# Late stages of a fused backward pass: TensorE in program order, w_down gradient products between the dh tiles, earlier head-group loads

## The chip, the core and the metric

One core of one Trainium2 chip. The metric is the time of one execution on the device in microseconds (us); unless said otherwise a number is the median of several executions. A change counts as faster or slower from 2% on. Different sets of runs were taken on different chips, each beside runs of the kernel before on the same chip.

## The reference

The reference is a forward pass and its gradients. Attention over given caches is multiplied by a gated layer:

```python
def _A_ref(x, k_cache, v_cache, wq, wo):        # 32 heads of 128, 2048 rows, D = 576
    q = (x @ wq).reshape(B, Sq, H, Dh).transpose(0, 2, 1, 3)
    scores = einsum("bhqd,bhkd->bhqk", q, k_cache) * (Dh ** -0.5)
    o = einsum("bhqk,bhkd->bhqd", softmax(scores), v_cache)
    return o.transpose(0, 2, 1, 3).reshape(B, Sq, H * Dh) @ wo

def _B_ref(x, w_gate, w_up, w_down):            # F = 4608
    g, u = x @ w_gate, x @ w_up
    return (_sigmoid(g) * u) @ w_down

xn = _layernorm(x)
out = x + _A_ref(xn, ...) * _silu(_B_ref(xn, ...))
# outputs: out, and the gradients of x, k_cache, v_cache, wq, wo, w_gate, w_up, w_down
```

(Shortened; the reference writes the matrix products as einsums and takes the gradients with a vector-Jacobian product.)

## The kernel before

The change concerns what follows attention. First come the output rows. Then 18 blocks of 256 columns of the gated layer each compute dh, from it du and dg, then the gradients of w_down, w_up and w_gate, and the block's share of the gradient of x (the "dx rows"). Last, eight groups of four heads compute the gradients of wq and wo and their share of dx; there the tiles are called dq, on and ds. In this part the instructions of SyncE, GpSimd and VectorE stay in the order in which the program names them; those of TensorE and ScalarE are placed by the scheduler of the language.

```python
with ..., tc.manual_schedule(engines={SP, Pool, DVE}):          # shortened
    ...
    for fb in range(NFB):                                       # 18 blocks
        ...
        for st in range(0, NT, G2):                             # 8 steps of two row tiles
            dh = ps.tile([P, G2, FB], f32, name="dh")           # pool of two buffers
            for g in range(G2):
                srows = slice((st + g) * P, (st + g + 1) * P)
                for i in range(DT):                             # 5: so 10 matmuls of 256 columns
                    nc.tensor.matmul(dh[:, g, :], lhsT=doBT[:, i, srows], rhs=wdT[:, i, :], ...)
            nc.vector.tensor_tensor(du_blk[:, sp_, :], dh[:], a_blk[:, sp_, :], op=ALU.mult)
            nc.scalar.mul(ndh[:], dh[:], -1.0)
            nc.vector.tensor_tensor(dg_blk[:, sp_, :], ndh[:], nbl[:, sp_, :], op=ALU.mult)
            if e % NTQ == 0:                                    # after each half:
                for k in range(2):                              # duT, then dgT
                    turn_rows(dugT[k], dug[k], e - NTQ, e, FBT) # a DMA transpose on SyncE
        if fb == NFB - 1:
            nc.gpsimd.dma_start(ds_all, rows_view(ds_d, 0, D))  # ds load, last block only
        for fl in range(FBT):                                   # two w_down products
            accumulate(psa.tile(...), h_blk, doB, slice(fl * P, (fl + 1) * P), dwd)
            nc.gpsimd.dma_start(out_8[r0:r0 + P, :], dwd[:])
        if fb == NFB - 1:
            load_on(onb0, 0)                                    # on load of head group 0
        ...                                                     # up and gate products, dx rows
```

`accumulate` runs 16 row tiles, each a pair of matmuls of 512 and 64 columns, and ScalarE copies the sum out. A head group starts like this:

```python
for hg in range(NHG):                                           # 8 groups
    if not final:
        load_on(onqs[(hg + 1) % 2][0], hg + 1)                  # loads of the next group
        load_dq(onqs[(hg + 1) % 2][1], hg + 1)
    nc.sync.dma_start_transpose(wqT, A_wq[:, cols])
    for a in range(NTE if final else 0, NT, NQ):
        turn_rows(dqbT, dqb, a, min(a + NQ, NT), HG)            # four DMA transposes
    if early:                                                   # group 6
        nc.sync.dma_start_transpose(wqT2[:], A_wq[:, (hg + 1) * HC:(hg + 2) * HC])
        turn_rows(dqbT2, onqs[(hg + 1) % 2][1], 0, NTE, HG)     # group 7's tiles, for joined rows
    wait_n = min(4 if early else 2, nsteps - 2)                 # products before the first row ending
    ...
```

## Time and profile before

| | before |
|---|---|
| time, median of 3 | 4979.05 us (4975.73 to 4979.33) |
| span of the profiled execution | 4981.3 us |
| TensorE busy | 4857.5 us, 98% |
| start of the late part | 3533.30 us |
| output rows | 148.69 us |
| blocks 1 to 16 | 49.31 us each |
| head groups 1 to 5 | 47.04 us each |

The profile is of one execution. PE is TensorE's matmuls and PEld its weight loads; DVE, ACT, POOL and SP are VectorE, ScalarE, GpSimd and SyncE. A name such as `dh<-wdT,doBT` means that tile dh was written from wdT and doBT; L1098 is line 1098 of the kernel. Brackets hold the idle time ahead of an instruction and what ended it. The prediction shows the lines that matter. One more view is needed, the queues around the last block, with start, length, engine and transfer. The block starts at 4520.01:

```profile
4534.27 6.12 SPq L1047 DMA_TRANSPOSE duT<-du_blk  x1
4540.47 20.42 SPq L1047 DMA_TRANSPOSE dgT<-dg_blk  x1
```

```profile
4532.93 1.16 POOL L1115 DMA_DIRECT2D doBT<-ds_d  x1 [22.26 <-PE dh L1098]
...
4539.64 1.17 POOL L1026 DMA_DIRECT2D doB<-on_d  x1
```

The second dgT transpose (0.5 MB) is issued 0.83 us after the on load (2048 rows of 512 values of 2 bytes, 2.1 MB) and holds its queue for 20.42 us.

### The profile page before, as it was taken

The numbers are of one execution on the slowest core, as the hardware profiler recorded it, in microseconds if no ns is written. First come the engines' busy times: TensorE is split into PE (matmuls) and PEld (weight loads), VectorE is DVE, ScalarE is ACT, GpSimd is POOL, SyncE is SP. The second block draws the span as 40 slices with busy tenths as digits, with TensorE's granted clock in tenths as the row PEclk, the third lists the DMA queues.
The fourth block names the chain that finished last, engine by engine and source line by source line (L and its number), as shares of the span: only waits on it lengthen the run. The fifth ranks groups of instructions, "written<-read, shape, count | busy, mean of one in ns | idle before, by whom it ended". The sixth has DMA issues, their size and how long they took to land.

```text
span 4981.3 us, 100870 instructions
## 1 busy us (share of the span) xinstructions
PE 4857.5 (98%) x40276; PEld 2897.3 (58%) x41029; DVE 2790.1 (56%) x6554; ACT 2473.1 (50%) x4228; POOL 840.7 (17%) x1330
## 2 busy tenths in 40 slices
PE   9999999999999999999999999999899999999998
PEld 4445666666666666666666666665455555555454
DVE  4544665666666566566566666666334545453225
ACT  4422766766766766666676676676221111111111
POOL 3322111111111111111111111111221111111111
PEclk9999999999999999999999999999999999999999
DMA  7887999999999999999999999999999999998765
GB/s 260 273 204 173 224 229 225 226 233 228 225 229 221 229 227 225 228 232 230 224 225 237 222 231 226 230 225 224 206 224 235 230 212 228 214 222 160 207 167 146
DMA packets 3048180, 1097.68 MB, mean 220 GB/s; under 512 B 2951889, under 2 KB 2956114, under 8 KB 3047698
## 3 DMA queue, kind: packets, MB, share of 16 engines
q1 hardware_dynamic: 2948930, 771.66, 82.5%
q0 software_dynamic: 98160, 318.85, 20.3%
q8 instruction: 322, 5.28, 0.4%
q14 instruction: 160, 1.31, 0.1%
q10 hardware_dynamic: 608, 0.59, 0.0%
HBM read 175.31 MB, written 177.93 MB: 71 GB/s over the span
## 4 chain that ended last, share of the span: by engine, by line
PE 88%; DVE 4%; issue 3%; DMA 3%; ACT 2%; SPq 1%; POOL 0%; ACTq 0%; POOLq 0%; DVEq 0%
PE acc L683 18%; PE acc L744 17%; PE acc L997 11%; PE sp L636 8%; PE dp L706 8%; PE acc L1052 8%; PE acc L215 6%; PE u_ps L450 3%; PE g_ps L448 3%; PE acc L533 3%; PE acc L957 2%; DVE du_blk L1101 1%; ACT ndh L1103 1%; PE acct L145 1%; DMA dST<-Pq 1%
## 5 line engine op out<-in xcount | busy, mean ns | idle before, releaser
L654 ACT ACTIVATE Pq<-sp 128x1024 bf16<-128x1024 f32 x1024 | 1046.9, 1023 | 262.3 <-PE sp L636 219.2
L709 DVE SCALAR_TENSOR_TENSOR Pq<-dp,negdelta,Pq 128x1024 bf16<-128x1024 f32 x512 | 654.8, 1279 | 46.8 <-PE dp L706 46.6
L712 ACT ACTIVATE t<-dp,negdelta 128x1024 bf16<-128x1024 f32 x512 | 567.1, 1114 | 214.9 <-PE dp L706 165.0
L683 PEld LDWEIGHTS <-dST 128*128 128x128 bf16 x8192 | 508.3, 98 | 157.4 <-DMA dST<-Pq 16.9
L706 PE MATMUL dp<-VT,dOT 128*128 128x512 bf16 x1919 | 581.6, 379 | 2.3
L683 PEld LDWEIGHTS <-PT 128*128 128x128 bf16 x8192 | 500.1, 98 | 128.7 <-DMA PT<-Pq 8.6
L683 PE MATMUL acc<-Kn,dST 128*128 128x128 bf16 x8192 | 557.5, 219 | 13.6 <-DMA dST<-Pq 11.7
L636 PE MATMUL sp<-KQ 128*128 128x512 bf16 x1858 | 567.8, 379 | 2.2 <-ACT Pq L654 2.1
L683 PE MATMUL acc<-Vn,PT 128*128 128x128 bf16 x8192 | 542.1, 219 | 6.4 <-DMA PT<-Pq 4.4
L744 PE MATMUL acc<-Pq,dOn 128*128 128x512 bf16 x1983 | 527.8, 379 | 10.2 <-issue 0.2
L713 DVE TENSOR_TENSOR Pq<-t,Pq 128x1024 bf16<-128x1024 bf16 x512 | 354.4, 692 | 321.1 <-ACT t L712 306.3
L744 PE MATMUL acc<-Pq,Qn 128*128 128x512 bf16 x2013 | 523.7, 379 | 4.9
L1142 DVE TENSOR_TENSOR dxn<-acc,dxn 128x576 f32<-128x576 f32 x272 | 206.0, 757 | 316.9 <-PE acc L1052 316.9
L724 ACT ACTIVATE dq_n<-acc,rsc 128x128 bf16<-128x128 f32 x512 | 187.5, 366 | 339.4 <-PE acc L683 317.9
L744 PEld LDWEIGHTS <-Qn 128*128 128x128 bf16 x2048 | 200.3, 98 | 240.9 <-issue 1.6
L744 PEld LDWEIGHTS <-dOn 128*128 128x128 bf16 x2048 | 199.0, 98 | 234.6 <-issue 1.3
L1103 ACT ACTIVATE ndh<-dh 128x512 bf16<-128x512 f32 x144 | 86.0, 597 | 420.0 <-DVE du_blk L1101 419.9
L636 PEld LDWEIGHTS <-KQ 128*128 128x128 bf16 x2048 | 179.0, 98 | 123.8 <-issue 3.1
L706 PEld LDWEIGHTS <-dOT 128*128 128x128 bf16 x2048 | 178.8, 98 | 124.1 <-issue 11.7
L641 DVE TENSOR_REDUCE rs_all<-rsp 128x1 f32<-128x2 f32 x512 | 78.4, 153 | 306.5 <-ACT Pq L654 295.3
L677 POOL DMA_DIRECT2D on_d<-o_n x128 | 97.1, 759 | 778.7 <-DVE junk L695 458.9
L677 POOL DMA_DIRECT2D dq_d<-dq_n x128 | 97.9, 765 | 721.8 <-ACT dq_n L724 682.0
(209 smaller groups left out, 6800.1 us busy)
## 6 DMA issues: line engine op xcount, KB each, us to landing
out_dram<-kvn POOLq DMA_DIRECT2D x64, 512.0 KB, 3.9
ah<-a_d POOLq DMA_DIRECT2D x18, 1024.0 KB, 9.0
ah<-h_d POOLq DMA_DIRECT2D x18, 1024.0 KB, 10.8
h_d<-h_row POOLq DMA_DIRECT2D x64, 256.0 KB, 3.5
a_d<-a_row POOLq DMA_DIRECT2D x64, 256.0 KB, 3.8
x_all<-in_A_k_cache_dram SPq DMA_DIRECT2D x64, 256.0 KB, 3.8
on_d<-o_n POOLq DMA_DIRECT2D x128, 128.0 KB, 4.6
kvT_d<-KQ POOLq DMA_DIRECT2D x32, 512.0 KB, 5.4
```

What stands on the lines that cost most here:

```text
L215: nc.tensor.matmul(av[:, :CH], lhsT=w[:, i, :], rhs=srcT[:, i, cs], start=(i == 0), stop=(i == DT - 1))
L636: nc.tensor.matmul(sp[:, c * CH:(c + 1) * CH], lhsT=hs.QT[:, qt * P:(qt + 1) * P], rhs=hs.KT[:, hf * HW_ + c * CH: hf * HW_ + (c + 1) * CH ...
L654: nc.scalar.activation(Pq[:, hsl], sp[:], AF.Exp, scale=SCALE, accum_out=hs.rsp[:, hf:hf + 1])
L683: nc.tensor.matmul(hs.acc[:, 0, :], lhsT=T[:, kt, :], rhs=rhs[:, kt, :], start=(kt == 0), stop=(kt == NT - 1))
L706: nc.tensor.matmul(dp[:, c * CH:(c + 1) * CH], lhsT=hs.dOT[:, qt * P:(qt + 1) * P], rhs=hs.VT[:, hf * HW_ + c * CH: hf * HW_ + (c + 1) * C ...
L709: nc.vector.scalar_tensor_tensor(Pq[:, hsl], dp[:], hs.negdelta[:, qt:qt + 1], Pq[:, hsl], op0=ALU.add, op1=ALU.mult)
L712: nc.scalar.activation(t[:], dp[:], AF.Identity, bias=hs.negdelta[:, qt:qt + 1], scale=1.0)
L713: nc.vector.tensor_tensor(Pq[:, hsl], t[:], Pq[:, hsl], op=ALU.mult)
L744: nc.tensor.matmul(self.acc, lhsT=self.nat[:, qt, :], rhs=self.slabs[qt][:, cs], start=(qt == self.lo), stop=(qt == self.hi - 1))
L997: nc.tensor.matmul(acc[:, n0:n0 + nn], lhsT=lhs[:, st, cols], rhs=rhs[:, st, n0:n0 + nn], start=(st == 0), stop=(st == NT - 1))
L1052: nc.tensor.matmul(acc[:, n0:n0 + nn], lhsT=lT, rhs=w[:, n0:n0 + nn], start=(k == 0), stop=(k == len(terms) - 1))
L1142: nc.vector.tensor_tensor(dxn[:, st, :], acc[:, :D], dxn[:, st, :], op=ALU.add)
```

## The change

The intent is to let TensorE work on w_down gradient products while VectorE and ScalarE digest a dh tile, and to begin each head group's loads as soon as their buffers are free. Its core:

```diff
-            tc.manual_schedule(engines={SP, Pool, DVE}):
+            tc.manual_schedule(engines={SP, Pool, DVE, PE}):
...
-        def accumulate(acc, lhs, rhs, cols, dst):
-            for st in range(NT):
+        def accumulate(acc, lhs, rhs, cols, dst, a=0, b=NT):
+            for st in range(a, b):
...
+                dwd_units = [(fl, st) for fl in range(FBT) for st in range(NT)]
+                def dwd_unit():          # one row tile of one w_down product
+                    ...                  # after the last: copy out and store
                 for st in range(0, NT, G2):
...
                     nc.vector.tensor_tensor(dg_blk[...], ndh[:], nbl[...], op=ALU.mult)
+                    for _ in range(FBT * G2):
+                        dwd_unit()
...
                 if fb == NFB - 1:
                     nc.gpsimd.dma_start(ds_all, rows_view(ds_d, 0, D))
-                for fl in range(FBT):
-                    ...                  # the two w_down products and their stores
+                while dwd_units:
+                    dwd_unit()
...
+            if NHG > 1:                  # ahead of the head groups
+                load_on(onqs[1][0], 1)
+                load_dq(onqs[1][1], 1)
...
-                if not final:            # at the head of a group
-                    load_on(onqs[(hg + 1) % 2][0], hg + 1)
-                    load_dq(onqs[(hg + 1) % 2][1], hg + 1)
...
-                if early:                # behind the four dqbT transposes
-                    nc.sync.dma_start_transpose(wqT2[:], ...)
-                    turn_rows(dqbT2, ...)
...
-                wait_n = min(4 if early else 2, nsteps - 2)
+                wait_n = min(5 if early else 2, nsteps - 2)
...
                     nc.sync.dma_start_transpose(dwq[:, :, lcols], dqTs[h % 2][:])
+                    if early and hl == min(1, HG - 1):
+                        nc.sync.dma_start_transpose(wqT2[:], ...)
+                        turn_rows(dqbT2, ...)
...
                 if not final:            # after a group's products
+                    if hg + 2 < NHG:
+                        load_on(onb, hg + 2)
+                        load_dq(dqb, hg + 2)
```

(Tile names and some arguments are shortened.) A consequence in the last block: the last w_down store is now emitted ahead of the ds load.

More of the change, by code (lines that the diff above doesn't have):

```diff
@@ L882 @@
     with late("pc") as pc, late("pcf") as pcf, \
-            tc.manual_schedule(engines={mybir.EngineType.SP, mybir.EngineType.Pool, mybir.EngineType.DVE}):
+            tc.manual_schedule(engines={mybir.EngineType.SP, mybir.EngineType.Pool, mybir.EngineType.DVE, mybir.EngineType.PE}):
         xn_all = pc.tile([P, NT, D], bf, name="xn_all")
@@ L998, in accumulate @@
                                      start=(st == 0), stop=(st == NT - 1))
-            alt.copy(dst[:, :D], acc[:, :D], eng="s")
+            if b == NT:
+                alt.copy(dst[:, :D], acc[:, :D], eng="s")
         def store_T(out_, cols, stg_):
@@ L1089 @@
                 du_blk, dg_blk = dug
+                dwd_units = [(fl, st) for fl in range(FBT) for st in range(NT)]
+                dwd_box = []
+                def dwd_unit():
+                    fl, st = dwd_units.pop(0)
+                    if st == 0:
+                        dwd_box[:] = [outp.tile([P, D], bf, name="dwd"), psa.tile([P, WD], f32, name="acc", tag="acc")]
+                    accumulate(dwd_box[1], h_blk, doB, slice(fl * P, (fl + 1) * P), dwd_box[0], st, st + 1)
+                    if st == NT - 1:
+                        r0 = fb * FB + fl * P
+                        nc.gpsimd.dma_start(out_8[r0:r0 + P, :], dwd_box[0][:])
                 for st in range(0, NT, G2):
@@ L1115 @@
                     nc.gpsimd.dma_start(ds_all, rows_view(ds_d, 0, D))
-                for fl in range(FBT):
-                    dwd = outp.tile([P, D], bf, name="dwd")
-                    accumulate(psa.tile([P, WD], f32, name="acc", tag="acc"), h_blk, doB, slice(fl * P, (fl + 1) * P), dwd)
-                    r0 = fb * FB + fl * P
-                    nc.gpsimd.dma_start(out_8[r0:r0 + P, :], dwd[:])
+                while dwd_units:
+                    dwd_unit()
                 if fb == NFB - 1:
@@ L1203 @@
                     turn_rows(dqbT, dqb, a, min(a + NQ, NT), HG)
-                if early:
-                    nc.sync.dma_start_transpose(wqT2[:], A_wq[:, (hg + 1) * HC:(hg + 2) * HC])
-                    turn_rows(dqbT2, onqs[(hg + 1) % 2][1], 0, NTE, HG)
                 dwq = wp.tile([P, DT, HC], bf, name="dwq")
@@ L1227 @@
                     nc.sync.dma_start_transpose(dwq[:, :, lcols], dqTs[h % 2][:])
+                    if early and hl == min(1, HG - 1):
+                        nc.sync.dma_start_transpose(wqT2[:], A_wq[:, (hg + 1) * HC:(hg + 2) * HC])
+                        turn_rows(dqbT2, onqs[(hg + 1) % 2][1], 0, NTE, HG)
                     if final and hl == HG - 1:
```

## The prediction

> **What bounds the kernel now.** I read the page first, then busy times by stage, then the timeline of TensorE, and last the waits of the queues. The page says that TensorE is the engine that matters:
>
> ```profile
> PE 4857.5 (98%) x40276; PEld 2897.3 (58%) x41029; DVE 2790.1 (56%) x6554; ACT 2473.1 (50%) x4228; POOL 840.7 (17%) x1330
> ```
>
> With 98% busy there can be no large gain from order alone. The change touches only what follows attention: a stage of output rows (about 3533 to 3682 us), 18 blocks of the gated-layer gradients (3682 to 4576) and 8 head groups (4576 to the end at 4981). So I looked for time lost there. One steady block is 4224.17 to 4273.47, 49.30 us, and the next ones repeat it to 0.01 us. Busy time of its three parts (dh with the w_down products; up and gate products; dx rows; columns: stretch, length, then PE, PEld, DVE, ACT, POOL, granted clock, DMA share, GB/s):
>
> ```profile
> 4224.17:4242.11 17.94, 17.37 (x143) 11.95 (x145) 11.62 (x22) 5.31 (x9) 0.56 (x1) 1.00 1.01 214
> 4242.11:4257.79 15.68, 15.58 (x128) 8.06 (x129) 2.24 (x4) 2.55 (x4) 2.93 (x5) 1.00 0.94 215
> 4257.79:4273.47 15.68, 15.52 (x127) 8.06 (x129) 11.36 (x15) 0.64 (x1) 4.76 (x6) 1.00 0.97 283
> ```
>
> Second and third part are dense: a pair of matmuls (512 and 64 columns) takes 0.245 us start to start (15.68 us / 64 pairs). A w_down, up or gate product over 16 row tiles is 16 pairs, 3.92 us; a dx row is 4 pairs, 0.98 us. A dh tile is 10 matmuls of 256 columns, 1.09 us (the first 20 of the block start 2.18 us before what follows). So the first part should be 8 x 1.09 + 2 x 3.92 = 16.56 us and takes 17.94: **1.38 us are lost per block**. The timeline of TensorE shows how:
>
> ```profile
> 4230.39 1.25 PE L1098 MATMUL dh<-wdT,doBT 128*128 128x256 bf16 x10
> 4231.48 0.65 PE L997 MATMUL acc<-doB,ah 128*128 128x64 bf16 x4
> 4232.14 1.25 PE L1098 MATMUL dh<-wdT,doBT 128*128 128x256 bf16 x10
> ...
> 4236.72 5.55 PE L997 MATMUL acc<-doB,ah 128*128 128x512 bf16 x43
> ```
>
> dh tiles come every 1.75 us with only about two pairs (0.49 us) between; 1.09 + 0.49 leaves some 0.17 us unused per tile, and the remaining w_down work is piled up at the end. The 1.75 us is the chain of VectorE and ScalarE, in program order on VectorE, with two dh buffers:
>
> ```profile
> 4227.22 0.68 DVE L1101 TENSOR_TENSOR du_blk<-dh,ah 128x512 bf16<-128x512 f32 x1
> 4228.62 0.42 DVE L1104 TENSOR_TENSOR dg_blk<-ndh,nbl 128x512 bf16<-128x512 bf16 x1 [0.72 <-ACT ndh L1103]
> 4228.96 0.68 DVE L1101 TENSOR_TENSOR du_blk<-dh,ah 128x512 bf16<-128x512 f32 x1
> ```
>
> Outside the blocks the chain breaks in three places: at the last block's dx rows, at group 0's dx rows, and in group 6, the last but one, where dx rows of two groups are joined:
>
> ```profile
> 4563.72 0.66 PE L1052 MATMUL acc<-wug,duT 128*128 128x512 bf16 x4 [2.08 <-DMA duT<-du_blk]
> 4566.56 0.74 PE L1052 MATMUL acc<-wug,dgT 128*128 128x64 bf16 x3 [2.18 <-DMA dgT<-dg_blk]
> ...
> 4612.41 17.51 PE L1052 MATMUL acc<-wdT,dqbT 128*128 128x512 bf16 x126 [4.71 <-ACT dqT L40]
> ...
> 4886.69 2.10 PE L1052 MATMUL acc<-wqT,dqbT 128*128 128x512 bf16 x8 [4.90 <-DMA dqbT<-dqb]
> ```
>
> Groups 1 to 5 are dense: 47.04 us each, which is 8 x 3.92 + 16 x 0.98.
>
> **What the Trainium skill says.** (1) "TensorE: Matmul & The Clock Gate", Part 2, step by step: matmuls keep program order, only weight loads are pulled ahead. The trace agrees: one weight load of the next dh tile runs at 4226.57, its other nine from 4226.89, when the tile's matmuls may start. So the emitted order is the whole lever. (2) "PSUM — Partial Sum Buffer", PSUM bank collisions: two engines must not touch one bank at once, so software keeps them apart. The trace agrees: ndh waits for du_blk although both only read dh (419.9 us of waiting in 142 places); the 1.75 us chain stays as it is. (3) The TensorE page, Part 1: after an idle window of about 3.4 us the clock falls to half until it has been busy as long. The trace agrees: after the 4.90 us wait eight matmuls take 1.92 us instead of 0.98. (4) "DMA: Bandwidth & Descriptors", Issuing engines are not separate DMA queues: all share 16 engines. The trace agrees: one dgT transpose issues in 1.98 us in the quiet first half of the last block, and holds its queue 20.42 us beside the ds and on loads.
>
> **The change part by part.**
> *w_down units among the dh tiles.* Work is neither added nor removed: 32 units of one pair, four after each dh tile. A step becomes 1.09 + 4 x 0.245 = 2.07 us, longer than the 1.75 us chain, so a dh buffer is free before TensorE needs it (du_blk, ndh and their handoffs take about 1.6 us after a tile's end; the tile two later starts 3.05 us after it). The old trace already shows such steps in block 0, at 3692.03, 3694.10 and 3696.17: 2.07 us. First part 16.56 us, block 47.92 us, saving 1.38 x 17 blocks = **23.5 us**. Block 0 has an extra VectorE multiply per step and gets nothing from me. The up product starts 0.98 us after the last dh tile and reaches the last rows some 3.4 us later, after du_blk; second-half transposes finish about 18 us after a block's start plus 4 us landing, against 40 us when dx needs them. Neither waits.
>
> *Last block.* It lost 22.54 - 15.68 = 6.86 us in its dx rows. The new order puts the last w_down store ahead of the ds load, so that load starts about 18 us into the block instead of 12.9; the second duT transpose (about 16.7) is then ahead of it, but dgT (about 18.3) still runs beside it. If dgT needs the 25.7 us it needed before, it lands at 44 where 40 is the need: half of the loss stays. I take **3.5 us** gain.
>
> *Group 0.* Loss now 4.71 us, plus 17.51 - 0.16 - 15.68 = 1.7 us at the low clock. The wait is named for ScalarE, but its cause is the queue: four dqbT transposes hold it for 32.58 us beside two 2 MB loads, and the dwq transposes behind them free dqT. Both loads are now emitted before the group. The on load was stuck behind the dwg store, which comes earlier when the last block's queue flows, so only one load would collide. I give it 60%: **4 us**.
>
> *Groups 1 to 5.* Already dense; the loads were issued during the previous group's dx rows at 4664, 4711, 4758 and are again. **0 us.**
>
> *Group 6.* Before, from its start 4864.96: transposes of both groups end at 19.1 us, and the join starts at 21.7. Now two dwq transposes (second ready at 12.6) come before the second set, so wqT2 goes out at about 15.8, dqbT2 at 18.0, and lands near 24.7, while TensorE is there after five products, 19.6. The wait stays about 5 us and the eight row endings on VectorE, 4.36 us each, start 3 us later: **2 us loss**. Group 7 and the tail: as before.
>
> *Output rows.* TensorE waits 10.5 us for a wo load and 3.5 us for the third oT; program order can use the first gap, but the third oT lands at the same time. **0 us.**
>
> Sum: 23.5 + 3.5 + 4 - 2 = 29 us; 4979 - 29 = **4950 us**, 0.6% less.
>
> **The rivals.**
> *DMA becomes the bound of the blocks.* For it: DMA share 0.92 to 0.99 in steady blocks, and a block 2.8% shorter would want up to 1.02. Against it: the same measure reaches 1.08 elsewhere, transposes land in 4 us, and TensorE waits for no DMA in any steady block. It would leave 0 to 10 us of the 23.5: 4963 to 4973.
> *Program order shows waits that the old order hid.* A wait in each block of 1.4 us would cancel everything: about 4975; a wait of 5 us in a few groups would cost 10 to 20 us: 4960 to 4970. For it: ScalarE is still ordered by the scheduler, and the join stands before data that may be late. Against it: the old order is nearly the program order already, outside the dh part.
> *The boundary stalls vanish altogether,* since transposes are now spaced differently: the 6.9, 6.4 and about 8 us (4.9 plus the slow clock) all go, 23.5 + 21 = 45 us: 4935.
>
> **Range and chances.** The 23.5 us is nearly arithmetic; the rest is -5 to +15 us of DMA timing. Range 4938 to 4963 us. Two per cent are 100 us, more than all idle time of TensorE in these stages, so faster by over 2% gets 0.01; slower by over 2% needs a stall of 7 us in every block, 0.01.
>
> **What would show it.** Right: steady block 47.92 us, dh steps of 2.07 us with eight matmuls between, no wait of L1098 for ndh; on load of group 1 before the last dx row ends; group 6 with a wait of some 5 us at its first joined row. Wrong: a block longer than 48.5 us, or TensorE waiting for duT, dgT, wug or wdT in steady blocks.

## The result, and the profile after

| | before | after |
|---|---|---|
| median | 4977.39 us (4 runs, 4973.89 to 4979.33) | 4948.19 us (4 runs, 4946.58 to 4964.82) |
| ratio | | 0.995, 95% interval 0.9927 to 0.9972 |
| profiled span | 4981.3 us | 4944.8 us |

The kernel after is 0.5% faster, which is within 2%: the class that had 0.98. The median is 1.8 us under the predicted 4950.

The page's busy time of the kernel after, with the same columns as before:

```profile
PE 4874.4 (99%) x41029; PEld 2893.5 (59%) x41029; DVE 2801.6 (57%) x6554; ACT 2474.9 (50%) x4228; POOL 842.3 (17%) x1330
```

The busy sums do not settle the matter: the trace before holds 40276 matmul records and this one 41029, so part of the 17 us rise on PE is records missing before. The stages do. A steady block of the kernel after, in its three parts (stretch, length, then PE, PEld, DVE, ACT, POOL, granted clock, DMA share, GB/s):

```profile
4206.89:4223.46 16.57, 16.57 (x147) 11.87 (x145) 9.27 (x16) 4.71 (x8) 1.08 (x2) 1.00 1.13 249
4223.46:4239.14 15.68, 15.68 (x131) 8.06 (x129) 5.24 (x9) 3.04 (x5) 1.63 (x3) 1.00 1.10 222
4239.14:4254.82 15.68, 15.68 (x131) 8.06 (x129) 11.36 (x15) 0.64 (x1) 6.03 (x8) 1.00 1.11 279
```

TensorE is busy in all of it. The 17.94 us of the first part have become 16.57, the others kept their 15.68. The timeline of TensorE shows the steps:

```profile
4208.96 1.26 PE L1110 MATMUL dh<-wdT,doBT 128*128 128x256 bf16 x10
4210.05 1.14 PE L997 MATMUL acc<-doB,ah 128*128 128x512 bf16 x8
4211.03 1.26 PE L1110 MATMUL dh<-wdT,doBT 128*128 128x256 bf16 x10
...
4223.46 2.83 PE L997 MATMUL acc<-xn_all,du_blk 128*128 128x512 bf16 x21
```

The dh tiles start 2.07 us apart, with eight matmuls between, and no w_down work is left over at the end. The chain of VectorE no longer sets the pace, since each du_blk now waits for TensorE:

```profile
4210.25 0.69 DVE L1113 TENSOR_TENSOR du_blk<-dh,ah 128x512 bf16<-128x512 f32 x1 [0.23 <-PE dh L1110]
4211.66 0.43 DVE L1116 TENSOR_TENSOR dg_blk<-ndh,nbl 128x512 bf16<-128x512 bf16 x1 [0.72 <-ACT ndh L1115]
4212.32 0.69 DVE L1113 TENSOR_TENSOR du_blk<-dh,ah 128x512 bf16<-128x512 f32 x1 [0.23 <-PE dh L1110]
```

What TensorE's matmuls and weight loads of dh tiles waited for, over the whole run, first before, then after (us, times):

```profile
  issue: 30.5, 104
  ACT ndh L1103: 4.0, 18
```

```profile
  issue: 2.1, 5
  ACT ndh L1115: 0.8, 2
```

"Issue" is a wait for nothing that the profile names; before it stood ahead of the second weight load of a dh tile, 104 times. It has all but gone with the waits for ndh.

In the last block, which now starts at 4494.48, the second pair of transposes is issued ahead of both loads (ds at 18.53 us into the block, on at 19.69), and dgT holds its queue for 3.97 us:

```profile
4511.00 1.43 SPq L1048 DMA_TRANSPOSE duT<-du_blk  x1
4512.52 3.97 SPq L1048 DMA_TRANSPOSE dgT<-dg_blk  x1
```

Group 6 got longer. In the kernel after it starts at 4824.66. A joined row is eight matmuls of group 6 (dqbT with the tile named wdT here) and eight of group 7 (with wqT). The first row's second half, which needs group 7's transposes, and the start of the next row:

```profile
4849.29 2.10 PE L1053 MATMUL acc<-wqT,dqbT 128*128 128x512 bf16 x8 [3.89 <-DMA dqbT<-dqb]
4851.21 1.85 PE L1053 MATMUL acc<-wdT,dqbT 128*128 128x512 bf16 x8
```

That is 24.63 us into the group, where before it was 4886.69 - 4864.96 = 21.73. The wait itself shrank, from 4.90 to 3.89 us. The group got longer at its end, where TensorE waits for the row endings on VectorE, which run later: once for 2.23 us and once for 2.79, against one wait of 1.68 before.

```profile
4887.14 5.56 PE L1053 MATMUL acc<-wdT,dqbT 128*128 128x512 bf16 x32 [2.79 <-DVE dxn L1256]
```

The eight matmuls take 4851.21 - 4849.29 = 1.92 us in place of 0.98, as they did before after 4.90 us of waiting. That again agrees with the clock behaviour which the prediction quotes from the Trainium skill: 3.89 us is a little over its idle window of about 3.4 us. The granted clock also shows where that short statement is too simple. The half-speed spell lasts 3.41 us here, but 6.83 us in group 6 of the kernel before. And in the dx rows of the kernel before, half speed set in at 4564.80 around two waits of 2.08 and 2.18 us with 0.66 us of work between them, neither of which is as long as the window.

All stages of these two profiles, and of three more of the same two kernels that the experiments gave (e10 and e12 are the kernel before again, e8 is the kernel after again), in us:

| stage | before | before, e10 | before, e12 | after | after, e8 |
|---|---|---|---|---|---|
| start of the late part | 3533.30 | 3530.30 | 3535.20 | 3532.07 | 3541.69 |
| output rows | 148.69 | 152.63 | 152.09 | 145.42 | 152.82 |
| block 0 | 49.12 | 49.13 | 49.13 | 50.06 | 50.07 |
| blocks 1 to 16 | 788.90 | 789.03 | 789.06 | 766.93 | 766.93 |
| block 17 to its dx rows | 33.63 | 33.64 | 33.64 | 32.26 | 32.26 |
| its dx rows | 22.54 | 16.86 | 15.68 | 15.68 | 15.68 |
| group 0 | 53.58 | 47.04 | 47.04 | 47.04 | 47.04 |
| groups 1 to 5 | 235.20 | 235.20 | 235.20 | 235.20 | 235.20 |
| groups 6, 7 and the tail | 116.34 | 116.77 | 116.46 | 120.14 | 119.91 |
| from the first dh tile to the end | 1299.31 | 1287.67 | 1286.21 | 1267.31 | 1267.09 |

Read from the first two profiles alone (before, after), blocks 1 to 16 gave 22 us, the last block's dx rows 6.9, group 0 6.5. The other columns correct that: the last two come and go in one and the same kernel.

### The profile page after: what moved, and what is told of

It is laid out like the page before. It is cut to its first block, busy times and chain, and to the rows that moved or that the text cites. A ratio compares the mean times of both kernels' runs of the same rounds, so it can differ in the third digit from the quotient of the medians.

```text
span 4944.8 us, 101626 instructions
## 1 busy us (share of the span) xinstructions
PE 4874.4 (99%) x41029; PEld 2893.5 (59%) x41029; DVE 2801.6 (57%) x6554; ACT 2474.9 (50%) x4228; POOL 842.3 (17%) x1330
## 5 line engine op out<-in xcount | busy, mean ns | idle before, releaser
L636 PE MATMUL sp<-KQ 128*128 128x512 bf16 x2048 | 609.7, 379 | 2.2 <-ACT Pq L654 2.1
L706 PE MATMUL dp<-VT,dOT 128*128 128x512 bf16 x2048 | 609.2, 379 | 2.3
```

Of the source, the lines that this page charges most:

```text
L636: nc.tensor.matmul(sp[:, c * CH:(c + 1) * CH], lhsT=hs.QT[:, qt * P:(qt + 1) * P], rhs=hs.KT[:, hf * HW_ + c * CH: hf * HW_ + (c + 1) * CH ...
L706: nc.tensor.matmul(dp[:, c * CH:(c + 1) * CH], lhsT=hs.dOT[:, qt * P:(qt + 1) * P], rhs=hs.VT[:, hf * HW_ + c * CH: hf * HW_ + (c + 1) * C ...
```

## The experiments

Twelve runs followed, all correct; e8, e10 and e12 are the kernel after or before once more. "Stages" below means the profile's stages as in the table.

| run | median us | its kernel before | ratio, 95% |
|---|---|---|---|
| e1_order_only | 5024.0 | 4979.0 | 1.0084 (1.0052 to 1.0116) |
| e2_blocks_only | 4945.9 | 4979.0 | 0.9928 (0.9896 to 0.9960) |
| e3_units_scheduled | 4951.97 | 4979.0 | 0.9937 (0.9905 to 0.9969) |
| e4_ds_late | 4973.99 | 4979.0 | 0.9984 (0.9951 to 1.0017) |
| e8_after_again | 4961.07 | 4977.43 | 0.9961 (0.9933 to 0.9988) |
| e5_ds_early | 4956.19 | 4977.43 | 0.9955 (0.9928 to 0.9982) |
| e6_join_early | 4947.04 | 4977.43 | 0.9932 (0.9904 to 0.9960) |
| e9_halves | 4935.95 | 4977.43 | 0.9913 (0.9883 to 0.9943) |
| e10_before_again | 4978.49 | 4980.22 | 0.9999 (0.9982 to 1.0016) |
| e7_on_late | 4979.5 | 4980.22 | 1.0004 (0.9987 to 1.0020) |
| e11_dgt_behind | 4962.97 | 4980.22 | 0.9967 (0.9951 to 0.9984) |
| e12_before_third | 4973.77 | 4982.77 | 0.9986 (0.9952 to 1.0020) |

### Which part of the change does the work

**e1, program order on TensorE alone:** the kernel before with

```diff
-            tc.manual_schedule(engines={SP, Pool, DVE}):
+            tc.manual_schedule(engines={SP, Pool, DVE, PE}):
```

> The kernel before with TensorE in program order and nothing else. My theory: the gain of the blocks comes from w_down pairs standing between the dh tiles, so without them TensorE waits for the 1.75 us chain of VectorE and ScalarE: last dh tile ends about 12.5 us into a block as before, the two w_down products (7.84 us) follow, first part 20.4 us, block about 51.7 us instead of 49.30, in all 4977 + 17 x 2.45 = about 5019 us. Rival, program order by itself is the gain: block 48 us, about 4950 us.

It is slower by 45 us in the medians, as expected. Blocks 1 to 16 take 51.77 us each and block 0 60.98. TensorE in a steady block:

```profile
4309.51 1.25 PE L1098 MATMUL dh<-wdT,doBT 128*128 128x256 bf16 x10 [0.38 <-ACT ndh L1103]
4311.26 1.25 PE L1098 MATMUL dh<-wdT,doBT 128*128 128x256 bf16 x10 [0.50 <-ACT ndh L1103]
...
4319.35 8.00 PE L997 MATMUL acc<-doB,ah 128*128 128x512 bf16 x62
```

The dh tiles again come every 1.75 us, now with nothing between, and the whole w_down work stands behind them. So 1.75 us is the pace of the chain through VectorE and ScalarE, and the scheduler's two pairs between the tiles had hidden part of it.

**e2, the blocks without the head-group part:** the kernel after with the loads, `wait_n` and the wqT2 and dqbT2 transposes of the head groups as before.

```diff
-            if NHG > 1:
-                load_on(onqs[1][0], 1)
-                load_dq(onqs[1][1], 1)
...
+                if not final:
+                    load_on(onqs[(hg + 1) % 2][0], hg + 1)
+                    load_dq(onqs[(hg + 1) % 2][1], hg + 1)
...
-                wait_n = min(5 if early else 2, nsteps - 2)
+                wait_n = min(4 if early else 2, nsteps - 2)
...                                       # wqT2 and dqbT2 back behind the dqbT transposes
```

> The change without its head-group part (loads of the groups, place of the joined transposes, and row start are as before); TensorE in program order, w_down pairs among the dh tiles. My theory: block 47.93 us; the last block and group 0 run dense (15.68 us of dx rows, 47.04 us) because of the block part alone; group 6 back to about 64.6 us from 67.9: about 4945 us, 3 below the full change. Rival, the loads moved by the head-group part freed group 0: group 0 waits 4 to 6 us again, 4951 to 4955 us.

Blocks 47.93 us, the last block's dx rows and group 0 together 62.7 as in the kernel after, groups 6, 7 and tail 115.11. The whole gain is in the blocks. The head-group part gives nothing and costs 120.14 - 115.11 = 5.0 us at the end in these two profiles; e3 below, with the same head groups as e2, took 117.0 there, so 3 to 5 us. The part holds three edits (loads, `wait_n`, place of the transposes), which e2 takes back together.

**e3, the same with TensorE left to the scheduler:** e2 with

```diff
-            tc.manual_schedule(engines={SP, Pool, DVE, PE}):
+            tc.manual_schedule(engines={SP, Pool, DVE}):
```

> As e2_blocks_only, but TensorE is left to the scheduler. The emitted order of TensorE in the blocks turns out to be the same. My theory: program order by itself brings nothing once the pairs are written between the tiles; block 47.93 us, within 3 us of e2_blocks_only, about 4945 us; only the first output rows are ordered otherwise. Rival, program order brings the 3.3 us seen in the output rows: those rows take 148.7 us here against 145.4 in e2_blocks_only.

Blocks 47.93 us as well. Once the w_down units are emitted between the tiles, the scheduler keeps them there, so fixing TensorE's order isn't needed for the gain. The time was 6 us above e2's, and the output rows took 154.87 us against 145.61. That is in the direction of the rival, but e5 and e6, with TensorE in program order, took 154.30 and 153.43 us there, so this doesn't show that program order speeds these rows up. One more line of this profile matters later. In the last block, which starts at 4504.07, dgT was issued at the same place as in the kernel after, 0.50 us ahead of the ds load, and yet:

```profile
4522.10 14.50 SPq L1048 DMA_TRANSPOSE dgT<-dg_blk  x1
```

### Where the last block's stall came from, and whether it was there

**e4, only the ds load moved:** the kernel before with the ds load behind the w_down stores.

```diff
-                if fb == NFB - 1:
-                    nc.gpsimd.dma_start(ds_all, rows_view(ds_d, 0, D))
                 for fl in range(FBT):
                     ...                  # w_down product and store
+                if fb == NFB - 1:
+                    nc.gpsimd.dma_start(ds_all, rows_view(ds_d, 0, D))
                 if fb == NFB - 1:
                     load_on(onb0, 0)
```

> The kernel before with one load moved: the ds load of the last block is issued after the two w_down stores instead of before them; TensorE's order is unchanged. My theory: the waits at the last block's dx rows (6.9 us with the low clock) and at group 0 (6.5 us) came from the ds load running ahead of the last du transpose, so both go: 4977 - 13 = 4964 us with blocks still 49.30 us. Rival, they went because of the denser blocks or because of the loads of the head groups: 4977 us, dx rows of the last block again 22 us.

Both transposes now go ahead of the loads: duT held its queue for 1.43 us (6.12 before), dgT, at 15.78 us into the block, for 3.20 (20.42 before). Dx rows 15.68, group 0 47.04, so the 13.4 us of stalls in the first profile are absent. But the time fell by only 5 us, with an interval that holds 0. The output rows took 154.61 us here, with the same instruction order on TensorE as before.

**e8, the kernel after again,** unchanged.

> The changed kernel once more, on the chip of the next three runs, to compare with them and to see how far its first output rows (145.4 us in its first profile) vary: 4948 us, stages 47.93 us a block, 47.04 us group 0, some 120 us from group 6 to the end. If the output rows vary by chance of transfer order they may take up to 150 us.

From the first dh tile to the end it repeats to 0.2 us (table above). The late part started 9.6 us later and the output rows took 152.82 us against 145.42. So the 3.3 us that the rows had "gained" were chance.

**e5, the ds load early in the new order:** the kernel after with the ds load behind the last dh tile instead of behind the last w_down store, 0.57 us ahead of the second duT transpose.

```diff
+                    if fb == NFB - 1 and st == NT - G2:
+                        nc.gpsimd.dma_start(ds_all, rows_view(ds_d, 0, D))
                     for _ in range(FBT * G2):
                         dwd_unit()
...
-                if fb == NFB - 1:
-                    nc.gpsimd.dma_start(ds_all, rows_view(ds_d, 0, D))
```

> The changed kernel with the ds load of the last block issued where the last dh tile frees its buffer (about 15.8 us into the block), ahead of the last duT transpose (16.5), as in the kernel before. My theory: duT then takes some 6 us to issue, dgT comes behind the on load (18.6) and takes some 20 us; the last block's dx rows take 20 to 23 us again and group 0 50 to 54: 4948 + 13 = 4961 us. Rival, the denser blocks or the earlier group loads removed these waits: 4948 us.

The expected stall did not come: dx rows 15.68, group 0 47.04. The transposes did slow down: duT held the queue for 12.93 us in place of 1.43, and dgT could only start at 29.53 us into the block and ended at 33.9. The second half of the dx rows needs it at about 40. A slow transpose is a stall only when its slack is used up.

**e7, the other load moved:** the kernel before with the on load of group 0 behind the first dwu stores, so that nothing is issued just ahead of the second dgT transpose.

```diff
-                if fb == NFB - 1:
-                    load_on(onb0, 0)
                 kv_store()
                 for (blk_, out_, nm) in (...):
                     ...
                     store_T(out_, fcols, stg_)
+                        if fb == NFB - 1:      # after nm == "dwu"
+                            load_on(onb0, 0)
```

> The kernel before with the on load of group 0 moved behind the first w_down gradient stores of the last block; everything else in its order. Theory (a transpose issued within a microsecond or so behind a 2 MB load goes slowly): the second dgT transpose, issued at about 20.5 us, now has no load close ahead of it and takes about 7 us in place of 20.4, so dx rows 15.7 and group 0 47.0: 13.4 us less in the profile's stages, ratio about 0.997. Rival (the ds load of 4 MB ahead is what slows it): the stall stays, dx 22 and group 0 53, ratio 1.000.

(The text calls the ds load 4 MB; by its shape, 2048 rows of 576 values of 2 bytes, it is 2.36 MB.) Dx rows 15.68 and group 0 47.04. The queue, in a block that starts at 4522.75:

```profile
4537.02 6.36 SPq L1047 DMA_TRANSPOSE duT<-du_blk  x1
4543.47 7.61 SPq L1047 DMA_TRANSPOSE dgT<-dg_blk  x1
```

With the ds load where it was and the on load away, dgT holds the queue for 7.61 us. That speaks for the on load just ahead of it as what made it slow, and against the ds load. In e1 too, dgT was issued ahead of the on load, 8 us behind the ds load, and held its queue for 7.02 us. But these are two profiles, and in e3 dgT took 14.50 us with both loads behind it, so the load just ahead is not the only cause. The time, however, did not move at all, and the next two runs give a reason.

**e10 and e12, the kernel before again,** unchanged, with a profile each.

> The kernel before once more, with a profile of its own: how far do the parts that my theory uses repeat? Theory: the stalls of the last block belong to the order in which its loads are issued and repeat: dx rows about 22.5 us, group 0 about 53.6, blocks 49.3 each, while the output rows (145 to 155 in the runs so far) and the start of the late part (3532 to 3544) are chance. Rival: the stalls of the last block are chance too, and dx rows or group 0 come at 15.7 and 47.0. Time within 0.4% of the kernel before.

> A third profile of the kernel before, unchanged. The first one lost 6.9 us in the last block's dx rows and 6.5 us in group 0; the second, of the same code, lost 1.2 us and 0.0. Theory formed on that: how long the transpose behind the 2 MB on load takes differs from execution to execution, near 20 us, around the 40 us at which dx needs it, so the loss lies anywhere from 0 to 13 us and a third profile will show dx rows between 15.7 and 22 us and group 0 mostly at 47.0. Rival: the second profile was the odd one, and dx rows are 22 and group 0 53 again. Blocks 1 to 16 at 49.31 us each in both.

The same two transposes, first of e10 (its block starts at 4521.09), then of e12 (4525.48):

```profile
4535.35 6.34 SPq L1047 DMA_TRANSPOSE duT<-du_blk  x1
4541.78 17.17 SPq L1047 DMA_TRANSPOSE dgT<-dg_blk  x1
```

```profile
4539.75 6.37 SPq L1047 DMA_TRANSPOSE duT<-du_blk  x1
4546.21 13.01 SPq L1047 DMA_TRANSPOSE dgT<-dg_blk  x1
```

One code, issued at the same moment of the block to within 0.3 us, and dgT holds the queue for 20.42, 17.17 and 13.01 us. TensorE in e10 waits only once in the dx rows:

```profile
4564.23 0.66 PE L1052 MATMUL acc<-wug,dgT 128*128 128x512 bf16 x4 [1.01 <-DMA dgT<-dg_blk]
```

That is 43.14 us into the block, 5.3 us after the queue was released at 37.86. In the first profile TensorE went on with dgT at 46.55, 5.7 us after the release at 40.88. An estimate from these for e12, 33.74 plus some 5.5, is 39; the dx rows need the tile at 33.64 + 8 x 0.98 + 0.49 = 41.97, and e12 has no wait. So the stall of 6.9 us in the dx rows, and the 6.5 us in group 0 behind it, belonged to that execution. The second run lost 1.2 us, the third nothing. Two of three profiles have no loss in group 0.

**e11, the slow place on purpose:** the kernel after with its second dgT transpose moved behind the first dwu transpose, thus 3.0 us behind the on load.

```diff
-                        for k in range(2):
+                        for k in range(1 if fb == NFB - 1 and e == NT else 2):
                             turn_rows(dugT[k], dug[k], e - NTQ, e, FBT)
...
                         nc.sync.dma_start_transpose(stg_[:, :, lcols], dwT[:])
+                        if fb == NFB - 1 and nm == "dwu" and fl == 0:
+                            turn_rows(dugT[1], dug[1], NT - NTQ, NT, FBT)
```

> The kernel after with the second dgT transpose of the last block moved behind the first dwu transpose, so that it is issued about 2 us behind the on load of group 0 in place of ahead of it. Theory: it goes slowly, ends past 40 us after the block's start, and dx rows take 18 to 25 us and group 0 up to 53 again: ratio to the kernel before about 0.996 to 0.998 where after again had 0.996 (so the stage times decide, not the time). Rival (slack or the free queue covers it, as in the run with ds early): dx 15.7 and group 0 47.0.

dgT, issued at 22.73 us, held the queue for 12.14 us in place of 3.97 in the kernel after. It was slow, as expected, but released at 34.87 instead of past 40: dx rows 15.68, group 0 47.04, no stall. The theory had the direction and missed the size, and the part of it that foretold a stall failed.

### Group 6, and a version that beats both

**e6, the joined rows fed earlier:** the kernel after with wqT2 transposed in group 5, and in group 6 the first half of dqbT, then dqbT2, and the second half of dqbT only after the second product.

```diff
-                for a in range(NTE if final else 0, NT, NQ):
+                for a in range(NTE if final else 0, NTE if early else NT, NQ):
                     turn_rows(dqbT, dqb, a, min(a + NQ, NT), HG)
+                if early:
+                    turn_rows(dqbT2, onqs[(hg + 1) % 2][1], 0, NTE, HG)
...
-                wait_n = min(5 if early else 2, nsteps - 2)
+                wait_n = min(4 if early else 2, nsteps - 2)
...
                     if early and hl == min(1, HG - 1):
-                        nc.sync.dma_start_transpose(wqT2[:], ...)
-                        turn_rows(dqbT2, ...)
+                        for a in range(NTE, NT, NQ):
+                            turn_rows(dqbT, dqb, a, min(a + NQ, NT), HG)
+                    if hg == NHG - 3 and hl == HG - 1:
+                        nc.sync.dma_start_transpose(wqT2[:], A_wq[:, (NHG - 1) * HC:])
```

> The changed kernel with group 6 fed in another order: wqT2 transposed in group 5, then wqT, the first half of dqbT, dqbT2, and the second half of dqbT after the second dwq transpose; joined rows start after four products. My theory: the joined rows start at about 16 us into group 6 instead of 24.6, without a wait, and the eight row endings on VectorE (4.36 us each) start 9 us earlier: group 6 takes 58 to 60 us instead of 67.9, from group 6 to the end 111 us instead of 120, 4939 us. Rival, the transposes are slow from contention and the wait only moves: 4945 to 4950 us.

The first joined row starts 15.67 us into the group and goes through without a wait (in the kernel after it started at 19.60 and waited in its middle until 24.63). Groups 6, 7 and tail take 109.62 us, against 119.91 in e8. One wait was left, at the end of group 6, for VectorE:

```profile
4898.54 3.81 PE L1053 MATMUL acc<-wdT,dqbT 128*128 128x512 bf16 x29 [2.23 <-DVE dxn L1260]
```

**e9, e6 with the row ending cut in two:** the last add of a row ending waits for ScalarE. It is now emitted behind the first half of the next row's ending, so VectorE does that in the meantime.

```diff
-                dx = sb.tile([P, D], bf, name="dx")
-                nc.vector.tensor_tensor(dx[:], t[:], gots.pop(st)[:], op=ALU.add)
-                nc.gpsimd.dma_start(o1[st * P:(st + 1) * P, :], dx[:])
+                done = finish_b()         # the add and the store of the row before
+                late_half.append((st, t))
+                return done
...
+                    if not todo_rows and late_half:
+                        finish_b()
```

> As e6_join_early, and the last add of each row's ending is issued on VectorE after the first part of the next row's ending, so that the 1.0 us wait for ScalarE's half is filled. My theory: a row's ending takes 3.4 us instead of 4.36, so 7 to 8 us less on VectorE in each of groups 6 and 7; group 6 then is bound by TensorE (55 to 57 us), the end by TensorE and the last stores (46 to 49 us after group 7 begins instead of 52): about 4933 us. Rival, VectorE was not the bound at the end: as e6_join_early.

Groups 6, 7 and tail take 102.09 us. Group 6 takes 54.88 us, exactly 8 x 3.92 + 8 x 1.96 + 8 x 0.98: eight products, eight joined rows, eight plain ones, with nothing between. Its end:

```profile
4877.23 4.08 PE L997 MATMUL acc<-doBT,doB 128*128 128x512 bf16 x32
4881.15 8.00 PE L1053 MATMUL acc<-wdT,dqbT 128*128 128x512 bf16 x64
4888.99 3.32 PE L997 MATMUL acc<-xn_all,dqb 128*128 128x512 bf16 x25
```

At 4935.95 us it is 25 us under the kernel after beside which it ran (e8, 4961.07) and 41 us under the kernel before: it beats both, by less than 1%.

## Why the prediction was right, and where it was not

The time was right: 4948.19 us against 4950, inside 4938 to 4963. So was e8's median, 4961.07. Step by step:

- **What bounds the kernel, and the lever:** right. e1 and e3 show that the place of the w_down work among the dh tiles decides the steady block, and that TensorE's program order by itself does not.
- **w_down units among the dh tiles, 23.5 us:** right. 789.0 - 766.93 = 22.1 us in blocks 1 to 16 and 33.64 - 32.26 = 1.4 us in the last one make 23.5. The steps are 2.07 us, the block 47.93 where 47.92 was said.
- **Block 0, "gets nothing from me":** wrong by 0.9 us. It lost that (49.13 to 50.06). I counted its extra VectorE multiply as a reason for no gain; in the new order dh tiles wait 0.19 and 0.62 us for ndh in its third and last step, and two steps between take 2.29 us, which fits the longer chain on VectorE; no run tests it.
- **Last block, 3.5 us, and group 0, 4 us:** wrong, and the failed step is "It lost 22.54 - 15.68 = 6.86 us" (and its like for group 0), which took one execution's stall for a property of the kernel. Profiles of the same code lost 1.2 us and nothing there. The queue that the prediction blamed for group 0, its four dqbT transposes, was held for 32.58 us in the first profile, but for 21.03 and 17.25 in the other two, whose group 0 is dense; and group 0 is dense in e2 with the group loads where they were. The working of the term failed as well: dgT was not slowed beside the ds load to land at 44 us but released its queue at 18.04 + 3.97 = 22.01, issued ahead of both loads (in e3, with the same order, at 32.53). Against the other two profiles of the kernel before, the term is 0 to 1.2 us. What the new order may give is slack: dx needs dgT at about 40, and in all eight profiles of kernels with the new blocks the queue was released by 34.9 and the last block's dx rows and group 0 together took 62.7 us, which is 15.68 + 47.04, even in e5 and e11, which slow the transposes on purpose. That the old order stalls more often in many executions is not shown.
- **Groups 1 to 5, 0 us:** right, 47.04 us in every profile.
- **Group 6, 2 us loss:** the mechanism was right, the size off. The joined half of the first row started 24.63 us into the group (24.7 was said for the landing of dqbT2), 2.9 us later than before, and groups 6, 7 and the tail lost 3.1 to 3.8 us. The text had found "start 3 us later" and then entered 2. The wait was 3.89 us where "about 5" was said. e2 shows that the loss belongs to the head-group part, and e6 that another order of the transposes (with `wait_n` back at 4) removes it; the other edits of that part were not tested alone.
- **Output rows, 0 us:** right in substance. In 14 profiles of all these kernels the rows took between 145.4 and 154.9 us, without a pattern that follows the code.

The sum with measured terms: 23.5 - 0.9 - 3.5 = 19 us, and 1286.21 - 1267.09 = 19.1 us is what e12 and e8 show from the first dh tile to the end. As a ratio, 19.1 us of 4979 is 0.9962, where the two timed pairs have 0.9950 and 0.9961. So the predicted 29 us were 21.5 us of lasting gain, of which 19 came, and 7.5 us taken from one execution's stall. That the sum came within 2 us was luck: the first timed pair differs by 29.2 us in the medians (25 in the means), the second by 16.4 (19 in the means). In the profiled pair that surplus lies in the stall of that one execution and in the start and length of the output rows. In the timed executions, which have no trace, where it lies stays open; that they spread by 5 to 30 us within one set of runs is measured.

Of the rivals, "DMA becomes the bound" is refuted: the DMA share rose to 1.10 to 1.13 in the block shown, and TensorE waited for none of it. "Waits that the old order hid" was true for group 6, and for block 0 by 0.9 us. "The boundary stalls vanish altogether" is what the first two profiles seemed to show, without its 21 us: 13.4 us vanished between them, two of three profiles of the kernel before hardly had them, and the third stall, in group 6, stayed.

Two things stay open. Why the same transpose in the same place takes 13 us once and 20 us another time, or 3.97 us in the kernel after and 14.50 in e3, was not found. Nor how often the kernel before stalls. If e7, whose profile has no stall, never stalls, then the kernel before loses on average at most what the interval of that pair allows; an estimate from its lower end, 0.9987, is 6.5 us.

## What to carry to other kernels

When a short chain on other engines paces small matmuls, spread independent matmul work in units between them so that one step of TensorE is longer than one step of the chain: here 2.07 against 1.75 us, which gave 1.38 us in each of 17 blocks, just as the arithmetic said. Before a stall of a few us at a stage's boundary is credited to a change, take a second profile of the old kernel. A stall caused by a transfer with little slack can differ from execution to execution, while the inner loops repeat to 0.02 us. A small transpose that others wait for is better issued ahead of large loads than just behind them: here 3.2 to 4.0 us of queue in six profiles against 13 to 20 in three. It is no guarantee, since a seventh took 14.50.

## What the Trainium skill lacked or had wrong

- "DMA: Bandwidth & Descriptors", Issuing engines are not separate DMA queues, says that all transfers interleave on the same 16 engines, and its section Latency and other measured facts gives 261 GB/s for a transpose on one kernel. Neither says what a transpose gets close behind a large plain load. Here a 0.5 MB transpose issued just ahead of the loads held its queue for 1.42 to 3.97 us, but once, in e3, for 14.50; issued about 1 us behind a 2.1 MB load it held it for 13.01, 17.17 and 20.42 us: 524288 bytes in 20.42 us are 26 GB/s.
- I found no page that says how far two executions of one kernel differ in DMA waits: one stage boundary lost 13.4, 1.2 and 0.0 us in three profiles of the same code, and the output rows took 145.4 to 154.9 us.
